# Holding TensorE's array mode longer, finishing a begun tile first, and one full-array product for the mask bias

## The chip, the cores and the metric

The kernel runs on one core of a Trainium2 chip. The metric is the device time of one execution in microseconds (us), taken as the median of the runs shown. A profiled execution stands beside them: it gives the instruction times from which everything below is read. The five engines are called PE (TensorE), DVE (VectorE), ACT (ScalarE), POOL (GpSimd) and SP (SyncE, which here only issues DMAs).

## The reference, cut to what matters

Four layers run one after the other on a sequence of 2048 rows of 512 numbers: A, B, A, B, each added to its own input. Layer A is attention over short segments with a memory that is handed from segment to segment; layer B is linear attention over the whole sequence.

```
def A(x, mem, ...):                       # layernorm before, residual after
    for s in range(64):                   # 64 segments of 32 rows
        h = concat(mem[8 rows], x[32 rows])
        q, k, v = h@Wq, h@Wk, h@Wv        # 32 heads of 128
        p = softmax(where(mask, q k^T * scale, -1e9))
        o = (p v) @ Wo
        mem = o[first 8 rows]             # goes into the next segment
        out = o[other 32 rows]
def B(x, ...):                            # linear attention, 32 heads of 16
    q, k, v = x@wqkv; phi(q), phi(k)
    out = (phi(q) (phi(k)^T v)) / (phi(q) sum phi(k)) @ wo
```

The mask lets the 8 memory rows see everything, and the others what is not later than they are. The chain that cannot be broken is the memory: segment s+1 cannot project its 8 memory rows before segment s has gone through projection, attention and output projection.

## The kernel before

**Work and staging.** All weights and x stay in SBUF. In layer A, "group" G is 128 rows (four segments, g = 0 to 3) and a segment s is one *turn* of the memory. Only 8+24 of a segment's 40 rows go through `project` in the turn; the last 8 rows of each of the four segments are collected into one "left-over" block of 32 rows, projected once per group by `left_block(G)`.

A projection (`project`, L630) uses the array as four independent 128x32 column strips: four products that run beside each other (here called a *pack*) and fill the 128 partitions of one PSUM bank with 8 heads by 4 strips. Four packs (one for each 128 input channels, c = 0 to 3) make a projection tile. `out_proj` (L808, eight packs) and the scores of the 32 segment rows (L759, L670) use the same strips. All this is called **column mode** below. Everything else on PE uses the array whole (**full mode**): transposes against the identity (L646), scores of the memory rows (L710), row sums by a product with ones (L722), probabilities times values (L735/L736 for the memory rows, L792/L793 for the others), the selection products L827 (picks the 8 memory rows out of the projected output and transposes them for the next turn) and L842/L847 (put segment rows back into place for the residual). The mask bias of the memory rows (`bias`, L701) is a third mode: two products with 16 of the 128 partitions contracted.

**A turn** is: project Q, K, V for two halves b = 0, 1; copy each tile out of PSUM into an image buffer `img` (`evac`, on ACT L498 or DVE L499); transpose it (L646) and copy it out again; bias, scores, exponential (L717, ACT), sums (L722), logarithm and exponential for the reciprocal (L725, L727, ACT), value products, multiply (L739, DVE); output projection (L808); copy; L827; copy into `hT`, from where the next turn's projections read. The 32 segment rows' attention (`x_attention`), the residual and the left-over block are filling work: nothing in the turn waits for them.

**What sets the order.** A list scheduler in the kernel (`_Prog.schedule`) writes each engine's order when the program is built. Each piece of work is a node with an assumed cost; `nd.tail` is the longest chain of assumed costs behind it. It steps through time, and on each engine takes the ready node with the largest tail. On PE it prefers a node of the mode that PE is in, as long as its tail is at most `MODE_SLACK` (0.3) below that of the best ready node; a switch is assumed to cost `PE_SWITCH` = 0.1. Nodes of a turn are `urgent`; a node that would open a new PSUM tile needs a free bank out of eight, and one that is not urgent needs three free. `after=early` on the bias ties it behind the copy of the K projection. On the chip the engines follow the written orders and wait for each other by semaphores; the assumed times are not used.

Image buffers: `img` has NI = 4 places, which `transposed` takes in turn for the memory turn and for the left-over block alike. The mask table `w16_sb` lies in a tensor of its own and is built once by POOL at the start (L542 to L547). Layer B lies in the same `arena` as layer A's buffers.

Of the kernel before, what the change touches and what calls it, by code (L numbers as in the profile page):

```python
# [18 lines left out]
MODE_SLACK = 0.3  # L19
# [35 lines left out]
class _Node:  # L55
    __slots__ = ("engs", "fn", "cost", "sync", "order", "tiles", "dsem", "dval", "eng", "start", "done",
                 "tail", "sig", "val", "waits", "know", "idx", "succ", "nleft", "urgent", "mode")


class _Prog:  # L60
# [17 lines left out]
    def add(self, engs, fn, cost, reads=(), writes=(), tiles=(), dsem=None, urgent=False, mode="full",  # L78
            after=()):
        nd = _Node()  # L80
        nd.mode = mode
        nd.engs = (engs,) if isinstance(engs, str) else tuple(engs)
# [12 lines left out]
        if dsem is not None:  # L95
            self.dma_tot[dsem] = self.dma_tot.get(dsem, 0) + 16
            nd.dval = self.dma_tot[dsem]
        for key in reads:
            st = self.res.setdefault(key, [None, []])
            if st[0] is not None:  # L100
                nd.sync.add(st[0])
            st[1].append(nd)
        for key in writes:
            st = self.res.setdefault(key, [None, []])
            if st[0] is not None and st[0] is not nd:
                nd.sync.add(st[0])
            for r in st[1]:
                if r is not nd:
                    nd.sync.add(r)
            st[0] = nd  # L110
            st[1] = []
        for tl in nd.tiles:
            if tl.ops:
                p = tl.ops[-1]
                if p.engs == ("pe",) and nd.engs == ("pe",):
                    nd.order.add(p)
                else:
                    nd.sync.add(p)
            tl.ops.append(nd)
        self.nodes.append(nd)  # L120
        return nd


    def schedule(self):
# [15 lines left out]
        for nd in reversed(nodes):  # L140
# [6 lines left out]
            nd.tail = best + min(nd.cost.values())  # L147
# [13 lines left out]
        n_left = len(nodes)  # L161
        pend = {e: [] for e in ENGINES}
# [34 lines left out]
        def pick_for(e):  # L197
            tn = self.now[e]
            while pend[e] and pend[e][0][0] <= tn + EPS:
                _, _, nd = heapq.heappop(pend[e])  # L200
                if nd.done is None:
                    heapq.heappush(ready[e], (-nd.tail, nd.idx, nd))
            pick = None
            kept = []
            while ready[e]:
# [4 lines left out]
                if first_of(nd):  # L210
                    bf = bank_for(tn)
                    if bf is None or bf[1] > tn + EPS or (not nd.urgent and n_free(tn) < 3):
                        kept.append(item)
                        continue
# [10 lines left out]
                elif nd.tail < pick.tail - MODE_SLACK:  # L225
# [12 lines left out]
        while n_left:  # L238
# [47 lines left out]
            nd.done = nd.start + nd.cost[e]  # L286
            self.now[e] = nd.done - (0.09 if e == "act" else 0.05 if e == "dve" else 0.0)
# [94 lines left out]
def _build_kernel(nc, A_x, A_mem0, A_Wq, A_Wk, A_Wv, A_Wo, A_seg_len, B_wqkv, B_wo, out):  # L382
# [35 lines left out]
    w16_sb = sb("w16_sb", [128, 4, 2, 32])  # L418
# [31 lines left out]
    img = av(NI * 512).rearrange("p (r x) -> p r x", r=NI)  # L450
# [14 lines left out]
    xlnA = av(D).rearrange("p (r x) -> p r x", r=1)  # L465

# [73 lines left out]

    BIG = -1.0e9
    pool(lambda g: g.memset(w16_sb[:, :, 0, :], 0.0), ["w16"])  # L542
    pool(lambda g: g.memset(w16_sb[:, :, 1, :], BIG), ["w16"])
    for gg in range(4):
        a = w16_sb[:, gg, 0, :]
        sel(a, GE, BIG, 0, [[-4, 4], [0, 8]], 1, "w16")
        sel(a, GE, BIG, 3, [[4, 4], [0, 8]], -1, "w16")  # L547
        sel(w16_sb[:, gg, 1, :], ALU.not_equal, 0.0, -gg, [[-4, 4], [0, 8]], 1, "w16")
# [71 lines left out]
    def a_layer(layer):  # L620
        img_no = [0]
# [68 lines left out]
        def mem_attention(s, b, early):  # L690
# [8 lines left out]
            def bias(pe):  # L699
                for a in range(2):  # L700
                    r = pe.matmul(tl.f32()[:, 128 * a:128 * a + 128], u16_sb[0:16, :],  # L701
                                  w16_sb[0:16, g, a, :].unsqueeze(1).to_broadcast([16, 4, 32]), start=(a == 0),
                                  stop=False, skip_group_check=True)
                return r
            add("pe", bias, c_pe(2, 128), reads=["u16", "w16"], tiles=[tl], urgent=True, after=early, mode="bias")
# [115 lines left out]
        def next_mem(s):  # L821
            G1, g1 = divmod(s + 1, 4)
            tl = P.tile()
            for h in range(2):
# [5 lines left out]
                add("pe", mm, c_pe(2, 128), reads=[(("outW", s % 3), h), "selm"], tiles=[tl], urgent=True)  # L830
# [5 lines left out]
        def residual(G, g):  # L836

            if g == 0:
# [5 lines left out]
                c_pe(1, 512), reads=[(("outW", w), 0), (("outW", w), 1), "selx"], tiles=[tl])  # L844
            if g == 3:
# [3 lines left out]
                    c_pe(1, 512), reads=[("outWl", 0), ("outWl", 1), "sell"], tiles=[tl])  # L849
# [195 lines left out]
```

## Time and profile before

| what | us |
|---|---|
| median of 3 runs | 2161.87 (2161.3 to 2163.71) |
| the profiled execution's own time | 2159.93 |
| its span, first to last instruction | 2158.2 |
| start until the first layernorm's transposes on PE | 48 |
| first layer A (48 to 1012) | 964 |
| first layer B (1012 to 1105) | 93 |
| second layer A (1105 to 2067) | 962 |
| second layer B (2067 to 2158) | 91 |

A view by stretches of time gives, for each, the busy time of every engine; a view of PE's instructions in order of time gives start and length of each row, with equal neighbours merged ("x8"). PE's matmuls overlap in the array, so the length of one is longer than the distance to the next: what a row costs is the distance from its start to the next row's start. In the four-group middle of a layer A the order repeats exactly every group.

### The profile page before, as it was taken

The numbers are of one execution on the slowest core, as the hardware profiler recorded it, in microseconds if no ns is written. First come the engines' busy times: TensorE is split into PE (matmuls) and PEld (weight loads), VectorE is DVE, ScalarE is ACT, GpSimd is POOL, SyncE is SP. The second block draws the span as 40 slices with busy tenths as digits, with TensorE's granted clock in tenths as the row PEclk, the third lists the DMA queues.
The fourth block names the chain that finished last, engine by engine and source line by source line (L and its number), as shares of the span: only waits on it lengthen the run. The fifth ranks groups of instructions, "written<-read, shape, count | busy, mean of one in ns | idle before, by whom it ended". The sixth has DMA issues, their size and how long they took to land.

```text
span 2158.2 us, 83024 instructions
## 1 busy us (share of the span) xinstructions
PE 2079.3 (96%) x37982; PEld 1163.5 (54%) x37982; DVE 1201.2 (56%) x3287; ACT 1159.7 (54%) x3112; POOL 14.8 (1%) x74
## 2 busy tenths in 40 slices
PE   1999999999999999998999999999999999999989
PEld 0555555555555555554655555555555555555545
DVE  0655555555554555556876555555555555554678
ACT  0555555555555555554645555555555555555554
POOL 2000000000000000000000000000000000000000
PEclk9999999999999999999999999999999999999999
DMA  9000000000000000001000000000000000000011
GB/s 350 3 3 2 3 3 3 3 3 3 3 3 3 3 3 3 3 3 41 1 2 3 3 3 3 3 2 3 3 3 3 3 3 3 3 3 3 3 41 40
DMA packets 12558, 30.48 MB, mean 14 GB/s; under 512 B 424, under 2 KB 9648, under 8 KB 10672
## 3 DMA queue, kind: packets, MB, share of 16 engines
q1 hardware_dynamic: 12208, 25.18, 3.2%
q8 instruction: 297, 4.87, 0.9%
q14 instruction: 53, 0.43, 0.1%
HBM read 23.08 MB, written 2.10 MB: 12 GB/s over the span
## 4 chain that ended last, share of the span: by engine, by line
PE 94%; DVE 2%; DMA 2%; ACT 1%; issue 0%; SPq 0%
PE pb L630 42%; PE pb L808 14%; PE pb L646 8%; PE pb L792 4%; PE pb L827 3%; PE pb L921 3%; PE pb L710 3%; PE pb L701 3%; PE pb L842 2%; PE pb L722 2%; DMA x_sb<-in_A_x_dram 2%; PE pb L735 2%; PE pb L759 2%; PE pb L914 1%; PE pb L736 1%; PE pb L771 1%
## 5 line engine op out<-in xcount | busy, mean ns | idle before, releaser
L498 ACT ACTIVATE arena_sb<-pb 128x512 bf16<-128x512 f32 (+6 forms) x1410 | 673.2, 492 | 458.7 <-PE pb L630 269.7
L630 PE MATMUL pb<-Wq_sb,arena_sb 128*32 128x512 bf16 x5120 | 478.2, 383 | 0.9 <-ACT arena_sb L498 0.4
L630 PE MATMUL pb<-Wk_sb,arena_sb 128*32 128x512 bf16 x5120 | 472.5, 382 | 0.0
L499 DVE CAST arena_sb<-pb 128x512 bf16<-128x512 f32 (+2 forms) x541 | 312.3, 578 | 237.6 <-PE pb L793 142.5
L630 PE MATMUL pb<-Wv_sb,arena_sb 128*32 128x512 bf16 x5120 | 374.4, 383 | 0.0
L808 PE MATMUL pb<-Wo_sb,arena_sb 128*32 128x512 bf16 x5184 | 350.1, 381 | 0.0
L780 DVE TENSOR_TENSOR arena_sb<-arena_sb 32x256 bf16<-32x256 bf16 x512 | 213.3, 417 | 133.6 <-ACT arena_sb L776 121.7
L499 DVE COPY arena_sb<-pb 128x512 bf16<-128x512 bf16 (+1 forms) x543 | 205.8, 399 | 137.8 <-PE pb L646 134.3
L646 PE MATMUL pb<-id_sb,arena_sb 128*128 128x128 bf16 x2560 | 216.7, 220 | 0.0
L630 PEld LDWEIGHTS pb<-Wq_sb,arena_sb 128*32 128x32 bf16 x5120 | 134.4, 96 | 133.2 <-ACT arena_sb L498 14.6
L646 PEld LDWEIGHTS pb<-id_sb,arena_sb 128*128 128x128 bf16 x2560 | 145.0, 97 | 103.2 <-issue 41.6
L630 PEld LDWEIGHTS pb<-Wk_sb,arena_sb 128*32 128x32 bf16 x5120 | 134.6, 97 | 108.5 <-issue 2.5
L717 ACT ACTIVATE arena_sb<-pb 128x256 bf16<-128x256 f32 x256 | 97.5, 381 | 158.9 <-PE pb L710 158.8
L498 ACT ACTIVATE outW_sb<-pb 128x256 fp32r<-128x256 f32 x198 | 75.8, 383 | 195.9 <-PE pb L808 194.5
L808 PEld LDWEIGHTS pb<-Wo_sb,arena_sb 128*32 128x32 bf16 x5184 | 119.7, 95 | 102.4 <-issue 20.7
L630 PEld LDWEIGHTS pb<-Wv_sb,arena_sb 128*32 128x32 bf16 x5120 | 109.6, 95 | 76.9
L782 DVE TENSOR_TENSOR arena_sb<-arena_sb 32x64 bf16<-32x64 bf16 x512 | 111.0, 217 | 15.8
L792 PE MATMUL pb<-arena_sb 128*128 128x128 bf16 x1024 | 115.2, 218 | 4.0 <-DVE arena_sb L782 4.0
L710 PE MATMUL pb<-arena_sb 128*128 128x32 bf16 x2048 | 118.6, 177 | 0.0
L499 DVE COPY arena_sb<-arena_sb 128x128 bf16<-128x128 bf16 x192 | 35.9, 194 | 128.8 <-PE pb L759 127.8
L793 PE MATMUL pb<-arena_sb 128*128 128x32 bf16 x1024 | 105.6, 178 | 0.0
L827 PEld LDWEIGHTS pb<-selm_sb,outW_sb 128*128 128x128 f32 x504 | 77.6, 188 | 51.8 <-ACT outW_sb L498 18.2
(108 smaller groups left out, 2330.6 us busy)
## 6 DMA issues: line engine op xcount, KB each, us to landing
Wq_sb<-in_A_Wq_dram SPq DMA_DIRECT2D x1, 4096.0 KB, 12.4
Wk_sb<-in_A_Wk_dram SPq DMA_DIRECT2D x1, 4096.0 KB, 22.2
Wv_sb<-in_A_Wv_dram SPq DMA_DIRECT2D x1, 4096.0 KB, 31.7
Wo_sb<-in_A_Wo_dram SPq DMA_DIRECT2D x1, 4096.0 KB, 43.2
arena_sb<-in_B_wqkv_dram SPq DMA_DIRECT2D x2, 1536.0 KB, 6.5
out_dram<-x_sb SPq DMA_DIRECT2D x16, 128.0 KB, 1.7
x_sb<-in_A_x_dram SPq DMA_DIRECT2D x1, 1920.0 KB, 11.5
arena_sb<-in_B_wo_dram SPq DMA_DIRECT2D x2, 512.0 KB, 7.5
```

Of the source, the lines that this page charges most:

```text
L498: return e.activation(o() if callable(o) else o, i() if callable(i) else i, ACTF.Copy)
L499: return e.tensor_copy(o() if callable(o) else o, i() if callable(i) else i)
L630: r = pe.matmul(tl.f32()[32 * j:32 * j + 32, 0:512], blk[:, c, :], W[:, c, o:o + 512], start=(c == 0), stop=(c == 3), tile_position=(0, 32 ...
L646: r = pe.transpose(tt.bf16()[:, 128 * i:128 * i + 128], img[:, k, 128 * i:128 * i + 128], id_sb[:, :])
L710: r = pe.matmul(tl.f32()[:, o:o + 32], kk[:, hh, :, :].rearrange("p j x -> p (j x)"), qT[:, r2, hh, :, 0:8], start=False, stop=True, skip_ ...
L717: add("act", lambda a: a.activation(Pm[:, k, :, :].rearrange("p a q -> p (a q)"), tl.f32()[:, 0:256], ACTF.Exp, scale=SCALE), c_act(256), ...
L780: add("dve", lambda v, q=q, j=j: v.tensor_tensor(Pbx[q, :, j, 0:32], Px[q, :, :], Rx[q, :, :], ALU.mult), c_dve(256), reads=["Px", "Rx"], ...
L782: add("dve", lambda v, q=q, j=j: v.tensor_tensor(Pbx[q, :, j, 32:40], PLL[q, g2, :, gl], Rx[q, :, 24:32], ALU.mult), c_dve(64), reads=[("P ...
L792: pe.matmul(o, vimg[:, r2, e], Pbx[:, hh, :, 0:32], start=True, stop=False)
L793: return pe.matmul(o[:, :, 24:32], vleft[:, g2, e], Pbx[:, hh, :, 32:40], start=False, stop=True)
L808: r = pe.matmul(tl.f32()[32 * j:32 * j + 32, :], oT[:, 4 * hh + j, :], Wo_sb[:, 8 * j + hh, :], start=(hh == 0), stop=(hh == 7), tile_posi ...
L827: r = pe.matmul(tl.f32()[:, 8 * c:8 * c + 8], outW[:, s % 3, 128 * c:128 * c + 128], selm_sb[:, :], start=True, stop=True)
```

## The change

1. `MODE_SLACK` goes from 0.3 to 2.0: PE may stay in its mode although a ready node of another mode has a chain that is up to 2.0 longer.
2. A node's rank is no longer its own tail alone (`prio`): a node gets at least the rank of the node before it on the same PSUM tile, so a projection, once begun, keeps the rank of its first pack.
3. The rule for opening a PSUM tile is rewritten: the oldest unopened tile needs one free bank, an urgent one two, any other three; a bank counts as free only when its last reader's signal has arrived.
4. The mask bias is one product over all 128 partitions and 256 columns instead of two with 16 partitions and 128 columns each; it counts as full mode. Its table `w16_sb` is now 128 by 4 by 2 by 128 numbers, lies in the arena and is built by POOL in each layer A.
5. The left-over block has two image buffers of its own; the memory turn keeps its four.
6. The assumed costs of L827 and of L842/L847 are raised (0.11 to 0.24 and 0.22 to 0.33). A field `lat` is added that nothing sets.

What is computed does not change.

```
-MODE_SLACK = 0.3
+MODE_SLACK = 2.0
...
+        for nd in nodes:
+            nd.prio = nd.tail
+            for tl in nd.tiles:
+                k = tl.ops.index(nd)
+                if k and tl.ops[k - 1] in nd.order and tl.ops[k - 1].done is None:
+                    nd.prio = max(nd.prio, tl.ops[k - 1].prio)
...
-                if own is None or (own.ops[-1].done is not None and own.ops[-1].done <= t_now):
+                lo = own.ops[-1] if own is not None else None
+                if lo is None or (lo.done is not None and lo.done + (PE_LAG if lo.eng == "pe" else HOP) <= t_now):
                     k += 1
...
-                    heapq.heappush(ready[e], (-nd.tail, nd.idx, nd))
+                    heapq.heappush(ready[e], (-nd.prio, nd.idx, nd))
...
-                    if bf is None or bf[1] > tn + EPS or (not nd.urgent and n_free(tn) < 3):
+                    while tiles[oldest[0]].bank is not None:
+                        oldest[0] += 1
+                    spare = 0 if tiles[oldest[0]] in nd.tiles else 1 if nd.urgent else 2
+                    if bf is None or bf[1] > tn + EPS or n_free(tn + EPS) <= spare:
...
-                elif nd.tail < pick.tail - MODE_SLACK:
+                elif nd.prio < pick.prio - MODE_SLACK:
                     kept.append(item)
                     break
...
-    img = av(NI * 512).rearrange("p (r x) -> p r x", r=NI)
+    img = av((NI + 2) * 512).rearrange("p (r x) -> p r x", r=NI + 2)
...
+    w16_sb = av(4 * 2 * 128).rearrange("p (g a h x) -> p g a h x", g=4, a=2, h=4)
...
-            k = img_no[0] % NI
-            img_no[0] += 1
+            k = img_no[0] % NI if urgent else NI + img_no[1] % 2
+            img_no[0 if urgent else 1] += 1
...
-            def bias(pe):
-                for a in range(2):
-                    r = pe.matmul(tl.f32()[:, 128 * a:128 * a + 128], u16_sb[0:16, :],
-                                  w16_sb[0:16, g, a, :].unsqueeze(1).to_broadcast([16, 4, 32]), start=(a == 0),
-                                  stop=False, skip_group_check=True)
-                return r
-            add("pe", bias, c_pe(2, 128), reads=["u16", "w16"], tiles=[tl], urgent=True, after=early, mode="bias")
+            add("pe", lambda pe: pe.matmul(tl.f32()[:, 0:256], u16_sb[:, :],
+                                           w16_sb[:, g, :, :, :].rearrange("p a h x -> p (a h x)"), start=True,
+                                           stop=False, skip_group_check=True),
+                c_pe(1, 256), reads=["u16", "w16"], tiles=[tl], urgent=True, after=early)
...
-                add("pe", mm, c_pe(2, 128), reads=[(("outW", s % 3), h), "selm"], tiles=[tl], urgent=True)
+                add("pe", mm, 0.24, reads=[(("outW", s % 3), h), "selm"], tiles=[tl], urgent=True)
...
+        BIG = -1.0e9
+        pool(lambda p: p.memset(w16_sb[:, :, 0, :, :], 0.0), ["w16"])
+        pool(lambda p: p.memset(w16_sb[:, :, 1, :, :], BIG), ["w16"])
+        for g in range(4):
+            sel(w16_sb[:, g, 0, :, :], GE, BIG, 0, [[0, 4], [-4, 4], [0, 8]], 1, "w16")
+            sel(w16_sb[:, g, 0, :, :], GE, BIG, 3, [[0, 4], [4, 4], [0, 8]], -1, "w16")
+            sel(w16_sb[:, g, 1, :, :], ALU.not_equal, 0.0, -g, [[0, 4], [-4, 4], [0, 8]], 1, "w16")
```

**How PE's order moves, place 1: the start of the attention in a turn of the steady part.** Rows are line, operation, output<-inputs, shape and count; "32x512" is column mode, everything else here full mode. `id_sb` marks a transpose, `w_sb,u_sb` the mask bias, "128x32" the memory rows' scores, `one_sb` their sums. Before:

```order
L646 MATMUL pb<-id_sb,arena_sb 128x128 x8
L630 MATMUL pb<-Wq_sb,arena_sb 32x512 x4
L630 MATMUL pb<-Wv_sb,arena_sb 32x512 x12
L701 MATMUL pb<-w_sb,u_sb 128x128 x2
L646 MATMUL pb<-id_sb,arena_sb 128x128 x4
L710 MATMUL pb<-arena_sb 128x32 x8
L630 MATMUL pb<-Wv_sb,arena_sb 32x512 x4
L630 MATMUL pb<-Wk_sb,arena_sb 32x512 x4
L646 MATMUL pb<-id_sb,arena_sb 128x128 x4
L722 MATMUL pb<-arena_sb,one_sb 128x128 x2
L630 MATMUL pb<-Wq_sb,arena_sb 32x512 x4
L630 MATMUL pb<-Wv_sb,arena_sb 32x512 x12
```

Now, at the same point of a turn (L639 is the old L630, L655 the old L646, L708 the bias, L716 the scores):

```order
L639 MATMUL pb<-Wk_sb,arena_sb 32x512 x16
L639 MATMUL pb<-Wv_sb,arena_sb 32x512 x32
L655 MATMUL pb<-id_sb,arena_sb 128x128 x8
L708 MATMUL pb<-arena_sb,u_sb 128x256
L655 MATMUL pb<-id_sb,arena_sb 128x128 x8
L716 MATMUL pb<-arena_sb 128x32 x4
L708 MATMUL pb<-arena_sb,u_sb 128x256
L639 MATMUL pb<-Wk_sb,arena_sb 32x512 x4
L716 MATMUL pb<-arena_sb 128x32 x12
```

Before, PE leaves the column mode three times in these rows besides the departure into the first one, and a fourth time into the second bias, which is the row behind them. Now it leaves it twice in a stretch that holds both biases: the value projections stand in one run of 32, and the transposes, the biases and the scores stand together.

**Place 2: the hand-over of the memory from one turn to the next.** `selm_sb,outW_sb` is the selection product L827 (now L833), after whose second pair and one copy the next turn's Q projection can start. Before:

```order
L808 MATMUL pb<-Wo_sb,arena_sb 32x512 x32
L759 MATMUL pb<-arena_sb 32x32 x32
L808 MATMUL pb<-Wo_sb,arena_sb 32x512 x12
L827 MATMUL pb<-selm_sb,outW_sb 128x8 x2
L808 MATMUL pb<-Wo_sb,arena_sb 32x512 x4
L827 MATMUL pb<-selm_sb,outW_sb 128x8 x2
L771 MATMUL pb<-arena_sb,bo_sb 128x256
L772 MATMUL pb<-arena_sb,bo_sb 128x8x8
L630 MATMUL pb<-Wq_sb,arena_sb 32x512 x4
L630 MATMUL pb<-Wk_sb,arena_sb 32x512 x4
L630 MATMUL pb<-Wq_sb,arena_sb 32x512 x4
```

Now (L814 is the old L808, L848 the old L842, L777/L778 the old L771/L772):

```order
L814 MATMUL pb<-Wo_sb,arena_sb 32x512 x32
L777 MATMUL pb<-arena_sb,bo_sb 128x256
L778 MATMUL pb<-arena_sb,bo_sb 128x8x8
L639 MATMUL pb<-Wk_sb,arena_sb 32x512 x8
L833 MATMUL pb<-selm_sb,outW_sb 128x8 x2
L639 MATMUL pb<-Wk_sb,arena_sb 32x512 x4
L848 MATMUL pb<-outW_sb,selx_sb 128x512
L833 MATMUL pb<-selm_sb,outW_sb 128x8 x2
L639 MATMUL pb<-Wk_sb,arena_sb 32x512 x8
L639 MATMUL pb<-Wq_sb,arena_sb 32x512 x16
```

The sums of the segment rows (L771/L772, now L777/L778) move ahead of the selection products, two packs of a left-over K projection stand between the last selection product and the next turn's Q projection, and the Q and K projections, which took turns pack by pack, now run one tile after the other.

Counted over the whole program, PE's order leaves the column mode 1,010 times before and 660 times now, and 256 pairs of bias products in the third mode become 256 single products in full mode.

More of the change, by code (lines that the diff above doesn't have):

```diff
@@ L56 @@
     __slots__ = ("engs", "fn", "cost", "sync", "order", "tiles", "dsem", "dval", "eng", "start", "done",
-                 "tail", "sig", "val", "waits", "know", "idx", "succ", "nleft", "urgent", "mode")
+                 "tail", "sig", "val", "waits", "know", "idx", "succ", "nleft", "urgent", "mode", "prio", "lat")
 class _Prog:
@@ L78, in add @@
     def add(self, engs, fn, cost, reads=(), writes=(), tiles=(), dsem=None, urgent=False, mode="full",
-            after=()):
+            after=(), lat=0.0):
         nd = _Node()
         nd.mode = mode
+        nd.lat = lat
         nd.engs = (engs,) if isinstance(engs, str) else tuple(engs)
@@ L146, in schedule @@
                     best = v
-            nd.tail = best + min(nd.cost.values())
+            nd.tail = best + min(nd.cost.values()) + nd.lat
+        for nd in nodes:
[4 more added lines that the diff above has]
+                    nd.prio = max(nd.prio, tl.ops[k - 1].prio)
         fenced = set()
@@ L161, in schedule @@
         n_left = len(nodes)
+        tiles = []
+        for nd in nodes:
+            for tl in nd.tiles:
+                if tl.ops[0] is nd:
+                    tiles.append(tl)
+        oldest = [0]
         pend = {e: [] for e in ENGINES}
@@ L285, in schedule @@
                 self.pe_mode = nd.mode
-            nd.done = nd.start + nd.cost[e]
-            self.now[e] = nd.done - (0.09 if e == "act" else 0.05 if e == "dve" else 0.0)
+            nd.done = nd.start + nd.cost[e] + nd.lat
+            self.now[e] = nd.start + nd.cost[e] - (0.09 if e == "act" else 0.05 if e == "dve" else 0.0)
             self.last[e] = nd
@@ L539, in _build_kernel @@
     sel(u16_sb[:, :], GE, 0.0, 7, [[-1, 128]], 8, "u16")
[L541 to L548, printed above, removed]
     pool(lambda g: g.memset(mx_sb[:, :], 1.0), ["mx"])
@@ L620, in a_layer @@
     def a_layer(layer):
-        img_no = [0]
+        img_no = [0, 0]
         cnt = {"m": 0}
@@ L843, in residual @@
                                            start=(g == 0), stop=False, skip_group_check=True),
-                c_pe(1, 512), reads=[(("outW", w), 0), (("outW", w), 1), "selx"], tiles=[tl])
+                0.33, reads=[(("outW", w), 0), (("outW", w), 1), "selx"], tiles=[tl])
             if g == 3:
```

3 lines of the change are left out of this document (1 added, 2 removed).

## The prediction

> **What bounds the kernel now.** First the page: its busy times, its slices and its chain.
>
> ```profile
> span 2158.2 us, 83024 instructions
> PE 2079.3 (96%) x37982; PEld 1163.5 (54%) x37982; DVE 1201.2 (56%) x3287; ACT 1159.7 (54%) x3112; POOL 14.8 (1%) x74
> ...
> PE 94%; DVE 2%; DMA 2%; ACT 1%; issue 0%; SPq 0%
> ```
>
> PE holds 94% of the chain that ended last; ACT and DVE are half empty. Since a busy PE need not be a PE at its peak, the stretches come next (columns: length, then busy time and count of PE, PEld, DVE, ACT, POOL, then clock).
>
> ```profile
> 48.00:1012.00 964.00, 961.01 (x18224) 531.99 (x18224) 521.34 (x1444) 532.00 (x1449) 0.00 (x0) 1.00 0.01 4
> 1012.00:1105.00 93.00, 79.69 (x774) 50.84 (x772) 79.52 (x201) 47.47 (x108) 0.21 (x2) 0.93 0.07 24
> 1105.00:2067.00 962.00, 959.18 (x18215) 530.38 (x18215) 520.88 (x1441) 531.59 (x1448) 0.00 (x0) 1.00 0.01 3
> ```
>
> The two layers A are 1926 of 2158 us, and PE lacks 3 us of busy time in each. The next row is one group, four turns, in the steady middle of the first layer.
>
> ```profile
> 183.20:243.10 59.90, 59.90 (x1142) 33.09 (x1138) 32.27 (x90) 33.55 (x91) 0.00 (x0) 1.00 0.01 3
> ```
>
> No gap at all, at full granted clock: 14.97 us a turn. The list of what PE waited for (total, times, longest) confirms it: its large rows are the start and layer B, and the largest one of a layer A is 4.0 us for two waits, at the layers' ends.
>
> ```profile
> PE pb L614 <- DVE arena_sb L607: 36.7, 4, 24.9
> PE pb L577 <- POOL arena_sb L524: 22.8, 1, 22.8
> ...
> PE pb L792 <- DVE arena_sb L782: 4.0, 2, 2.0
> ```
>
> So in a layer A time is what PE's rows cost one after the other, and a shorter row of rows is a shorter layer, until a wait appears.
>
> **What a change of mode costs.** These rows, in order of time, are from a turn of the first layer; a row's cost is the distance to the next start.
>
> ```profile
> 310.18 0.39 PE L630 MATMUL pb<-Wq_sb,arena_sb 128*32 128x512 bf16 x4
> 310.40 0.39 PE L630 MATMUL pb<-Wk_sb,arena_sb 128*32 128x512 bf16 x4
> 310.72 0.62 PE L646 MATMUL pb<-id_sb,arena_sb 128*128 128x128 bf16 x8
> 311.27 0.83 PE L630 MATMUL pb<-Wv_sb,arena_sb 128*32 128x512 bf16 x12
> 312.04 0.28 PE L701 MATMUL pb<-w_sb,u_sb 16*128 16x128 bf16 x2
> 312.25 0.40 PE L646 MATMUL pb<-id_sb,arena_sb 128*128 128x128 bf16 x4
> 312.48 0.25 PE L710 MATMUL pb<-arena_sb 128*128 128x32 bf16 x4
> 312.59 0.38 PE L646 MATMUL pb<-id_sb,arena_sb 128*128 128x128 bf16 x4
> 312.81 0.25 PE L710 MATMUL pb<-arena_sb 128*128 128x32 bf16 x4
> 312.99 1.05 PE L630 MATMUL pb<-Wv_sb,arena_sb 128*32 128x512 bf16 x16
> ...
> 314.30 0.27 PE L722 MATMUL pb<-arena_sb,one_sb 128*128 128x128 bf16 x2
> 314.41 0.25 PE L710 MATMUL pb<-arena_sb 128*128 128x32 bf16 x4
> ```
>
> A pack followed by a pack costs 0.22 (310.18 to 310.40); followed by a transpose it costs 0.32. Leaving the column mode is 0.10. Four transposes followed by full-mode work cost 0.22 (312.59 to 312.81), so eight 0.44; the eight before the V projection cost 0.55: the return is 0.11. Four score products cost 0.11 (312.48 to 312.59), but 0.18 before a projection: that return is 0.07. A round trip is thus 0.17 to 0.21, and I take 0.19. The bias pair costs 0.21 (312.04 to 312.25), the pair of sums, which has the same columns but stands in full mode, 0.11 (314.30 to 314.41): going from the bias mode to the full mode costs another 0.10. The way into the bias mode costs the same 0.10 or so as any departure (three packs, 311.27 to 312.04, are 0.77 where 3 x 0.22 are 0.66).
>
> The Trainium skill, TensorEngine Tiling (Array Packing), section Tiling Modes, says that changing the tiling mode drains the engine; TensorE: Matmul & The Clock Gate, section Step-by-step, puts that drain at about 128 cycles, an estimated 0.053 us at its 2.4 GHz. By that price the mode term below would be 350 x 0.106 + 254 x 0.053 = 51 us instead of 91. The rows show about twice the price at each of three kinds of change, so I go by the rows.
>
> **The change, part by part.** *Fewer changes of mode.* The order leaves the column mode 1,010 times now and 660 times after: 350 x 0.19 = 66 us, between 60 (at 0.17) and 74 (at 0.21). *The bias in full mode.* 254 of its 256 pairs stand between column and full mode: 254 x 0.10 = 25 us, between 23 and 28. The way in was counted above. Together 91, between 83 and 102.
>
> *The product itself.* One of 256 columns with 128 partitions contracted: the nearest row is L771, also 256 columns.
>
> ```profile
> 306.91 0.28 PE L771 MATMUL pb<-arena_sb,bo_sb 128*128 128x256 bf16 x1
> 307.03 0.19 PE L772 MATMUL pb<-arena_sb,bo_sb 128*128 128x64 bf16 x1
> ```
>
> It costs 0.12 against 0.11 for the pair in full mode: 256 x 0.01 = 3 us lost at most. Nor does each removed change give its mean: a selection product with four-byte operands hides part of one behind its long weight load. Going along the new order row by row, with each pair of neighbours at the distance that the same pair has in the trace (pairs that do not occur by the nearest kind), eight turns come to 114.7 us where two groups of before are 119.8: 5.1 us, and over 16 such stretches 82. I take 84, nearer to this than to 91, since it holds all pairs.
>
> *The order of finishing tiles, the bank rule, more mode slack.* They cost no rows; they shift when ACT and DVE get their work, and so can open waits. The hops that matter are at the end of a turn, where the tail of the layer shows one with nothing in between:
>
> ```profile
> 991.58 0.55 PE L827 MATMUL pb<-selm_sb,outW_sb 128*128 128x8 f32 x4
> ...
> 992.38 0.18 DVE L499 CAST arena_sb<-pb 128x32 bf16<-128x32 f32 x1
> ...
> 992.62 0.40 PE L630 MATMUL pb<-Wq_sb,arena_sb 128*32 128x512 bf16 x4 [0.15 <-DVE arena_sb L499]
> ```
>
> 0.25 from the product's end (992.13) to the copy, 0.18 copy, 0.06 to PE. The last selection product starts about 0.25 before its end, so its start and the next projection must be at least 0.74 apart, or some 0.6 where the quicker hop of the middle applies. In the new order the hand-over has two packs behind the last selection product: 0.18 + 0.43 = 0.61. That is at the edge; it costs 0 to 0.13 a turn. Going through the other waits of the steady part in the same way (producer's row, hop, time of the rows between), I find one in eight turns short by 0.23 and three by 0.03; near the layers' ends some of 0.2 to 0.7, as long as those there before. 16 x 0.3 = 5 us, and 3 for layer B, whose order also changes at places where DVE and ACT are behind: 8 us. The low end is 0; the high end, 0.3 a turn for queues on ACT and DVE that such a count does not see, is 128 x 0.3 = 38 us.
>
> *Left-over image buffers.* PE's list of waits has no row in layer A for an image buffer that was still in use: 0. Without the two places the left-over copies would share the four of the turn; what that would cost the trace does not show.
>
> *The mask table.* POOL builds it anew behind each layer B: two fills and 12 selections of 128x128.
>
> ```profile
> L524 POOL TENSOR_SCALAR_AFFINE_SELECT u_sb<-u_sb 128x128 bf16<-128x128 bf16 x2 | 0.6, 292 | 0.1
> L559 POOL MEMSET arena_sb<- 128x480 bf16 x1 | 0.5, 498 | 0.1
> ...
> 1117.23 0.28 PE L701 MATMUL pb<-w_sb,u_sb 16*128 16x128 bf16 x2
> ```
>
> 12 x 0.29 + 2 x 0.5 = 4.5 us, from 1105 on, while the projections of the first left-over block and turn run until the first bias at 1117.2: hidden with 7 us to spare, and POOL has nothing else queued there. Without this cover it would be 4.5 us, once. At the start POOL's list is ahead of x by far (the first layernorm product waits until 48 us for x).
>
> *The sum.* 2158.2 - 84 + 8 = 2082.2 us of span; the profiled execution's own time was 1.7 above its span: 2083.9. The runs' median is 1.9 above the profiled execution: **2086 us**. Own range: 2158.2 - 102 + 3.6 = 2060 if everything goes to the good end, 2158.2 - 80 + 38 + 3.6 = 2120 at the other; 2066 to 2112 is what I hold for this case.
>
> **Rivals.** *Half the gain goes into short waits* (chance 0.13, 2112 to 2140). Runs of 32 or 48 products of one mode leave copies in bunches: six projection tiles end within 5.2 us, and a copy takes 0.69 on DVE and 0.60 on ACT. For it: in the new order more waits have little room than before, and PE's order is fixed, so that it cannot do something else meanwhile. Against it: tiles that finish one after the other, each 0.87 us (four packs), give two copiers an even supply, where Q and K used to end 0.22 apart; ACT and DVE are 55% busy. At 0.33 us a turn it takes 42 us: 2086 + 34 = 2120.
>
> *The mode switch is cheaper when left out than it looks* (0.05): pairs overlap, only about half the price is saved, 2158.2 - 46 + 8 + 3.6 = 2124. Against it: the distances above are between starts on a PE without gaps. The price that the skill's drain gives, 51 us, ends near the same place, 2119.
>
> *PE is not the bound* (0.03, no change). Overlapping matmuls could look busy while something else sets their pace; PE would then only show gaps where the changes of mode were, and the time would stay at 2162. For it: weight loads keep PE's array for only 33.09 of a group's 59.90 us. Against it: the starts of the rows above follow from the rows themselves (0.22 a pack, 0.055 a transpose), and no wait ends in between. The Trainium skill, Perfetto Trace Analysis, section Identifying the Most-Contended Engine, has the rule that speaks for this rival: matmul busy time misjudges PE, and LDWEIGHTS busy, here 54%, shows its headroom.
>
> *The memory chain becomes the bound and the kernel gets slower* (0.05). Its rows (mean ns is the second number after the bar):
>
> ```profile
> L499 DVE COPY arena_sb<-pb 128x512 bf16<-128x512 bf16 x491 | 195.4, 420 | 136.0 <-PE pb L646 134.3
> L499 DVE CAST arena_sb<-pb 128x512 bf16<-128x512 f32 x283 | 194.9, 689 | 88.4 <-PE pb L630 83.7
> L717 ACT ACTIVATE arena_sb<-pb 128x256 bf16<-128x256 f32 x256 | 97.5, 381 | 158.9 <-PE pb L710 158.8
> L725 ACT ACTIVATE arena_sb<-pb 128x128 f32<-128x128 f32 x256 | 70.3, 275 | 56.1 <-PE pb L722 52.9
> L727 ACT ACTIVATE arena_sb<-arena_sb 128x128 f32<-128x128 f32 x256 | 80.1, 313 | 2.1
> L739 DVE TENSOR_TENSOR arena_sb<-pb,arena_sb 128x128 bf16<-128x128 f32 x256 | 74.1, 290 | 54.9 <-PE pb L736 51.0 <-PE pb L793 0.3 <-PE pb L722 0.2
> ```
>
> Copies and attention 2.4, the copies of the output (an estimate of 0.4 for 256 columns, from 0.69 for 512) and of the memory (0.18, above); on PE 16 packs of Q and K (3.5), the last four of the output projection (0.9), products between (0.6); some ten hops of 0.06 to 0.4, together 2: about 10 us of the 14.97. Holding a mode lets a ready link wait while up to 2.0 of rank difference is served. The chain crosses the mode border at four places a turn (projection to transposes, values to output projection, that to selection, selection to projection). From a mean hold of 1.2 us at each of them (10 + 4.8 = 14.8) it would end every turn later than PE's rows do; at 1.5 us it is 16.0 a turn, 128 x 1.0 above before: 2290. For it: a run of 32 V products (1.7 us) now stands ahead of the first transposes of a turn. Against it: the holds at the other borders are one or two packs, 0.2 to 0.4.
>
> **Chances and range.** Forecast 0.74, short waits 0.13, half price 0.05, no change 0.03, slower 0.05. The range 2064 to 2122 holds the forecast's case nearly whole and about half of the next two. A measurement of this kernel tells 0.2% (4 us) from no change. Faster: 0.74 + 0.13 + 0.05 = 0.92; same 0.03; slower 0.05.
>
> **What would show it.** The group of four turns at 57 to 58 us (two successive ones need not be alike) with PE still without gaps; eight transposes behind a projection still at 0.32 and 0.55 of distance; the new bias product at 0.12 among transposes; PE's waits in a layer A below 10 us in all; layer B at 91 to 95 us; POOL's second table done before the first bias of the second layer A. Wrong, if PE's waits within the layers A sum to over 40 us, if a change of mode costs something else where runs are long, or if a turn shows PE waiting for the copy behind the selection product each time.

## The result and the profile after

The changed kernel takes **2074.18 us** (median of 4 runs, 2072.74 to 2077.47), the kernel before 2161.59 (2160.55 to 2163.71): ratio 0.9597, 95% interval 0.958 to 0.9613, so 4.0% faster. The forecast was 2086 with a range of 2064 to 2122. One execution of another kernel below (the ring of six image buffers) took 4735 us with PE's rows over twice as long; it was the one with the profile, so that kernel is told by its other runs' times alone.

The page of the changed kernel: busy times and the chain that ended last, as shown of before.

```profile
span 2073.7 us, 82319 instructions
PE 1979.0 (95%) x37726; PEld 1188.5 (57%) x37726; DVE 1049.7 (51%) x3117; ACT 1305.0 (63%) x3282; POOL 23.6 (1%) x88
...
PE 89%; DVE 5%; DMA 2%; ACT 2%; issue 1%; SPq 0%; DVEq 0%
```

PE is still the engine that ends last, but its share of the chain fell from 94% to 89%, and DVE and ACT now hold 7%: turns have begun to wait for copies. Work also moved between the two copying engines, which no edit asks for: ACT from 1160 to 1305 us, DVE from 1201 to 1050. The stretches (length, busy time and count of PE, PEld, DVE, ACT, POOL, then clock):

```profile
48.00:967.60 919.60, 909.86 (x18096) 543.28 (x18096) 445.60 (x1359) 604.89 (x1534) 0.00 (x0) 1.00 0.01 4
967.60:1062.30 94.70, 79.53 (x777) 51.12 (x781) 79.71 (x201) 47.40 (x109) 3.69 (x10) 0.95 0.07 23
1062.30:1981.50 919.20, 909.91 (x18087) 542.77 (x18087) 444.61 (x1356) 604.30 (x1532) 2.50 (x7) 0.99 0.01 3
1981.50:2073.70 92.20, 79.38 (x769) 51.13 (x769) 75.87 (x193) 46.35 (x104) 0.21 (x2) 0.94 0.14 47
260.56:374.10 113.54, 112.89 (x2259) 67.50 (x2259) 56.24 (x172) 74.91 (x191) 0.00 (x0) 1.00 0.01 3
```

The layers A went from 964.0 to 919.6 and from 962.0 to 919.2, together 87 us; the layers B are 1.7 and 1.0 longer. The last row is eight turns of the steady part: 113.54 us, where before has 119.8. The order repeats every eight turns now, no longer every four.

What a change of mode costs has not changed. PE's rows in order of time (start, length, row), at the start of a turn's attention:

```profile
254.34 1.04 PE L639 MATMUL pb<-Wk_sb,arena_sb 128*32 128x512 bf16 x16
255.21 1.90 PE L639 MATMUL pb<-Wv_sb,arena_sb 128*32 128x512 bf16 x32
257.04 0.62 PE L655 MATMUL pb<-id_sb,arena_sb 128*128 128x128 bf16 x8
257.50 0.27 PE L708 MATMUL pb<-arena_sb,u_sb 128*128 128x256 bf16 x1
257.53 0.48 PE L848 MATMUL pb<-outW_sb,selx_sb 128*128 128x512 f32 x1
257.85 0.23 PE L798 MATMUL pb<-arena_sb 128*128 128x128 bf16 x1
```

Eight packs of V cost 1.83 from their start to the next row's (8 x 0.216 = 1.73 and one departure, 0.10). Eight transposes cost 0.46, without a return to the column mode behind them, and the bias starts without a change of mode ahead of it.

PE's waits, the largest ones (total, times, longest):

```profile
PE pb L798 <- DVE arena_sb L788: 4.4, 4, 2.0
PE pb L639 <- DVE arena_sb L517: 3.6, 12, 0.3
PE pb L853 <- DVE outWl_sb L517: 3.6, 12, 0.5
...
PE pb L728 <- ACT arena_sb L723: 1.7, 2, 0.9
PE pb L814 <- DVE arena_sb L745: 1.6, 6, 0.4
```

Two waits are new in the steady part, each once in eight turns: those of L639 and of L853 for a copy by L517. The first is at the hand-over of the memory:

```profile
265.78 0.59 PE L833 MATMUL pb<-selm_sb,outW_sb 128*128 128x8 f32 x4
266.23 0.48 PE L848 MATMUL pb<-outW_sb,selx_sb 128*128 128x512 f32 x1
266.35 0.71 DVE L788 TENSOR_TENSOR arena_sb<-arena_sb 32x64 bf16<-32x64 bf16 x3
266.63 0.40 PE L639 MATMUL pb<-Wq_sb,arena_sb 128*32 128x512 bf16 x4
267.09 0.19 DVE L517 CAST arena_sb<-pb 128x32 bf16<-128x32 f32 x1
267.32 0.22 DVE L788 TENSOR_TENSOR arena_sb<-arena_sb 32x64 bf16<-32x64 bf16 x1
267.34 0.83 PE L639 MATMUL pb<-Wq_sb,arena_sb 128*32 128x512 bf16 x12 [0.31 <-DVE arena_sb L517]
```

The selection product ends at 266.37, but the copy of the memory (L517, 128x32) stands behind three multiplies on DVE and starts at 267.09. PE issues one pack of a left-over projection and then nothing until 267.34. The bracket says 0.31 idle; the distance of the starts is 0.71 where a pack takes 0.22, so PE lost 0.49. The pack's row is 0.40 long, so the first 0.18 behind those 0.22 lie under it and do not show as idle time. The second is in front of the left-over output's selection product:

```profile
373.56 0.25 PE L716 MATMUL pb<-arena_sb 128*128 128x32 bf16 x4
373.63 0.41 DVE L517 CAST outWl_sb<-pb 128x256 fp32r<-128x256 f32 x1
374.10 0.50 PE L853 MATMUL pb<-outWl_sb,sell_sb 128*128 128x512 f32 x1 [0.28 <-DVE outWl_sb L517]
```

By idle time PE lacks 9.7 us in each layer A now (919.6 less 909.86), where before it lacked 3. Since short waits hide, I count waiting by distances too: for each row and its next, what exceeds the usual distance of that row before that mode (the 30th percentile over all kernels here) by more than 0.015 us. This gives 10 us in each layer A before and 19 after; in eight steady turns 0.7 and 1.3. How rows are merged and where the usual distance is set shifts all these levels together by some 4 us a layer; the differences between kernels are what is used below.

### The profile page after: what moved, and what is told of

It reads as the page before. It is cut to its first block, busy times and chain, and to the rows that moved or that the text cites. A ratio compares the mean times of both kernels' runs of the same rounds, so it can differ in the third digit from the quotient of the medians.

```text
span 2073.7 us, 82319 instructions
## 1 busy us (share of the span) xinstructions
PE 1979.0 (95%) x37726; PEld 1188.5 (57%) x37726; DVE 1049.7 (51%) x3117; ACT 1305.0 (63%) x3282; POOL 23.6 (1%) x88
## 4 chain that ended last, share of the span: by engine, by line
PE 89%; DVE 5%; DMA 2%; ACT 2%; issue 1%; SPq 0%; DVEq 0%
PE pb L639 42%; PE pb L814 13%; PE pb L655 7%; PE pb L798 3%; PE pb L935 3%; PE pb L833 3%; PE pb L716 2%; DVE arena_sb L786 2%; PE pb L848 2%; DMA x_sb<-in_A_x_dram 2%; PE pb L728 2%; PE pb L765 2%; PE pb L1002 1%; PE pb L928 1%; ACT arena_sb L516 1%; DVE arena_sb L788 1%
## 5 line engine op out<-in xcount | busy, mean ns | idle before, releaser
L516 ACT ACTIVATE arena_sb<-pb 128x512 bf16<-128x512 f32 (+6 forms) x1604 | 825.4, 519 | 451.9 <-PE pb L639 284.6
L517 DVE COPY arena_sb<-pb 128x512 bf16<-128x512 bf16 (+1 forms) x520 | 201.3, 407 | 529.5 <-PE pb L655 525.5
L639 PE MATMUL pb<-Wq_sb,arena_sb 128*32 128x512 bf16 x5120 | 351.4, 382 | 3.6 <-DVE arena_sb L517 3.6
L639 PE MATMUL pb<-Wk_sb,arena_sb 128*32 128x512 bf16 x5120 | 353.9, 382 | 0.6 <-ACT arena_sb L516 0.4
L814 PE MATMUL pb<-Wo_sb,arena_sb 128*32 128x512 bf16 x5184 | 337.1, 384 | 1.6 <-DVE arena_sb L745 1.6
L639 PE MATMUL pb<-Wv_sb,arena_sb 128*32 128x512 bf16 x5120 | 319.6, 380 | 0.0
L517 DVE CAST arena_sb<-pb 128x128 bf16<-128x128 f32 (+3 forms) x370 | 157.9, 429 | 137.4 <-PE pb L799 50.6
L639 PEld LDWEIGHTS pb<-Wv_sb,arena_sb 128*32 128x32 bf16 x5120 | 139.3, 97 | 129.4
L639 PEld LDWEIGHTS pb<-Wk_sb,arena_sb 128*32 128x32 bf16 x5120 | 138.6, 97 | 125.9 <-issue 2.4
L655 PE MATMUL pb<-id_sb,arena_sb 128*128 128x128 bf16 x2560 | 210.0, 220 | 0.0
L639 PEld LDWEIGHTS pb<-Wq_sb,arena_sb 128*32 128x32 bf16 x5120 | 129.0, 96 | 125.4 <-issue 12.7
L814 PEld LDWEIGHTS pb<-Wo_sb,arena_sb 128*32 128x32 bf16 x5184 | 126.8, 96 | 115.0 <-issue 10.9
L655 PEld LDWEIGHTS pb<-id_sb,arena_sb 128*128 128x128 bf16 x2560 | 151.4, 97 | 69.6 <-ACT arena_sb L516 48.8
L798 PE MATMUL pb<-arena_sb 128*128 128x128 bf16 x1024 | 124.5, 217 | 5.9 <-DVE arena_sb L788 4.4
L716 PE MATMUL pb<-arena_sb 128*128 128x32 bf16 x2048 | 110.0, 177 | 0.1
L716 PEld LDWEIGHTS pb<-arena_sb 128*128 128x128 bf16 x2048 | 81.8, 96 | 34.7 <-DVE arena_sb L517 14.9
L833 PEld LDWEIGHTS pb<-selm_sb,outW_sb 128*128 128x128 f32 x504 | 75.0, 189 | 46.0 <-ACT outW_sb L516 27.1
```

What stands on the lines that cost most here:

```text
L516: return e.activation(o() if callable(o) else o, i() if callable(i) else i, ACTF.Copy)
L517: return e.tensor_copy(o() if callable(o) else o, i() if callable(i) else i)
L639: r = pe.matmul(tl.f32()[32 * j:32 * j + 32, 0:512], blk[:, c, :], W[:, c, o:o + 512], start=(c == 0), stop=(c == 3), tile_position=(0, 32 ...
L655: r = pe.transpose(tt.bf16()[:, 128 * i:128 * i + 128], img[:, k, 128 * i:128 * i + 128], id_sb[:, :])
L716: r = pe.matmul(tl.f32()[:, o:o + 32], kk[:, hh, :, :].rearrange("p j x -> p (j x)"), qT[:, r2, hh, :, 0:8], start=False, stop=True, skip_ ...
L798: pe.matmul(o, vimg[:, r2, e], Pbx[:, hh, :, 0:32], start=True, stop=False)
```

## The experiments

Theory: time goes by the number of changes of the array's shape, 0.19 us for each departure from the column mode with its return and 0.08 to 0.10 for each change between bias and full mode; what PE waits comes on top. The rivals are told with each run. Departures are counted in the written order; "bias changes" are those between bias and full mode. Twelve kernels ran, four at a time on one chip beside the kernel before, which took 2161.8 each time.

| kernel | departures | bias changes | median us | ratio to before, 95% |
|---|---|---|---|---|
| before | 1,010 | 256 | 2161.6 | |
| before, bias in full mode | 1,006 | 0 | 2137.85 | 0.9888 (0.9871 to 0.9904) |
| before, slack 2.0 | 860 | 256 | 2131.56 | 0.986 (0.9843 to 0.9876) |
| changed | 660 | 0 | 2074.18 | 0.9597 (0.958 to 0.9613) |
| changed, bias of 16 partitions | 660 | 418 | 2110.27 | 0.9762 (0.9747 to 0.9776) |
| changed, slack 0.3 | 770 | 0 | 2105.07 | 0.9735 (0.972 to 0.9749) |
| changed, no finishing of tiles | 806 | 0 | 2102.44 | 0.9727 (0.9713 to 0.9742) |
| changed, old assumed costs | 678 | 0 | 2076.89 | 0.9609 (0.9595 to 0.9624) |
| changed, ring of four images | 626 | 0 | 2082.45 | 0.963 (0.9616 to 0.9645) |
| changed, ring of six images | 600 | 0 | 2080.21 | 0.9618 (0.9602 to 0.9634) |
| changed, DVE costs | 666 | 0 | 2079.71 | 0.9618 (0.9604 to 0.9633) |
| changed, slack 6.0 | 620 | 0 | **2062.76** | 0.9538 (0.9523 to 0.9554) |
| changed, DVE costs, slack 6.0 | 620 | 0 | 2062.15 | 0.9538 (0.9523 to 0.9552) |
| changed, DVE costs, ring of six, slack 4.0 | 572 | 0 | 2069.32 | 0.9566 (0.9552 to 0.958) |

**The third mode put back into the changed order.** All rows stand where they stood; only the number of partitions that the bias contracts differs.

```
-            ... u16_sb[:, :], w16_sb[:, g, :, :, :] ...
+            ... u16_sb[0:16, :], w16_sb[0:16, g, :, :, :] ...
```

> The changed kernel with its order untouched, but the one bias product of 256 columns contracts only the first 16 partitions (the others are zero, so the sum is the same). Theory (a change of the array's shape costs time, whatever the product's size): all 256 biases come from full-mode work in this order and 162 of them go back to it; entering costs 256 x 0.09 to 0.10, leaving to full mode 162 x 0.09 to 0.10, leaving to a projection was paid already: +38 to +42 us, about 2114 us. Rival (what was saved was the second product and the order around it, not the shape): 2074, within 4 us of the changed kernel.

Measured 2110.27, 36 us more. The same place of a turn in this kernel, PE's rows in order of time:

```profile
260.78 0.62 PE L655 MATMUL pb<-id_sb,arena_sb 128*128 128x128 bf16 x8
261.33 0.28 PE L708 MATMUL pb<-arena_sb,u_sb 16*128 16x256 bf16 x1
261.54 0.49 PE L848 MATMUL pb<-outW_sb,selx_sb 128*128 128x512 f32 x1
261.87 0.23 PE L798 MATMUL pb<-arena_sb 128*128 128x128 bf16 x1
```

From the transposes to the next value product are 1.09 us where the changed kernel has 0.81 (257.04 to 257.85), 0.28 for two changes at this place; on the mean over all 418 changes, 36 us are 0.09 each. A product that contracts 16 partitions among full ones is a mode of its own and is paid on the way in and out; the rival is out.

**The bias alone, in the order of before.** Two products as before, but all partitions and full mode.

```
-  ... u16_sb[0:16, :], w16_sb[0:16, g, a, :] ..., mode="bias")
+  ... u16_sb[:, :], w16_sb[:, g, a, :] ...)
```

> The kernel before with one edit: its two bias products contract all 128 partitions and count as full mode; 1,006 departures from the column mode instead of 1,010, and no third mode. Theory (shape): 254 changes from bias to full mode at 0.09 to 0.10 saved, 4 round trips at 0.19: 24 to 26 us less, 2136 us. Rival (shape is free, only the halved number of products matters): 2161, within 4 us of before.

Measured 2137.85, 24 us less, with as many products as before. So the gain of this edit is the shape; that one product took the place of two is not needed for it.

**Slack alone, in the kernel before.**

```
-MODE_SLACK = 0.3
+MODE_SLACK = 2.0
```

> The kernel before with the mode slack at 2.0 as its only edit. By its order 860 departures from the column mode instead of 1,010 (58 of them into the bias mode), 100 changes from full to bias mode instead of 2, 156 from bias to full instead of 254. Theory (changes): 150 x 0.19 = 28 us less, the bias changes even out: 2133. Rival (without finishing begun tiles a longer hold keeps tiles open and the chain late): 2150 or more, with PE's waits in the layers A above 15 us.

Measured 2131.56, 30 us less, near the count of 28, although waiting in a layer A is 16 us against 10.

**Slack undone in the changed kernel.** `MODE_SLACK` is 0.3 again, all other edits stay.

> The changed kernel with the mode slack back at 0.3. By the written order PE leaves the column mode 770 times instead of 660. Theory (number of changes): 110 x 0.19 = 21 us more, 2095 us. Rival (the slack costs as much in waits as it saves in changes): within 5 us of 2074, with fewer waits of PE in the layers A than the 11 or so of the changed kernel.

Measured 2105.07, 31 us more where the count says 21. The slack of 0.3 does not wait less: eight steady turns have 2.2 us of waiting (1.3 in the changed kernel), and PE's list has

```profile
PE pb L853 <- ACT outWl_sb L516: 8.4, 28, 0.3
PE pb L798 <- DVE arena_sb L788: 8.0, 34, 1.2
```

so these orders do not trade changes against waits; each order has its own waits. Over a whole layer A its waiting is only about 1 us above that of the changed kernel, so waits do not explain most of the 10 us above the count.

**No finishing of begun tiles.**

```
-                    nd.prio = max(nd.prio, tl.ops[k - 1].prio)
+                    pass
```

> The changed kernel with the rank of a node its own tail alone, as before: a begun tile is not finished first. By the written order 806 departures from the column mode instead of 660. Theory of changes alone: 146 x 0.19 = 28 us more, 2102. With waits at the rate of the run with slack 0.3 (31 us for 110 departures, 0.28 each): 2115. Rival (finishing tiles pays by earlier copies, not by changes): above 2120.

Measured 2102.44: the count to the microsecond. This edit works by the changes it avoids. That it is met so exactly is partly luck: this order waits some 4 us less in each layer A than the changed kernel, and its rows cost as much more than the count.

**Old assumed costs of the selection products.**

> The changed kernel with the old assumed costs of the selection products (0.11 and 0.22). By the written order 678 departures instead of 660: theory of changes alone 3 us more, 2077. Rival (the assumed costs matter by themselves: with too low ones the order asks for work before it is ready): over 2082, with PE's waits before the next turn's first projection (on the copies of ACT or DVE) above 10 us in all.

Measured 2076.89, as by the count. The difference to the changed kernel, 2.7 us, is within what these runs tell.

**Image buffers.** Shared by the turn and the left-over block: as before with four (`% NI`), and with all six (`% (NI + 2)`, shown here).

```
-            k = img_no[0] % NI if urgent else NI + img_no[1] % 2
-            img_no[0 if urgent else 1] += 1
+            k = img_no[0] % (NI + 2)
+            img_no[0] += 1
```

> The changed kernel, but the six image buffers are one ring that the turn's projections and the left-over block share. By the written order PE leaves the column mode 600 times instead of 660. Theory (time goes by the number of changes): 60 x 0.19 = 11 us less, 2063 us. Rival (buffers of their own keep the left-over block's copies out of the turn's way): PE's waits in the layers A grow by 10 us or more and the time is 2074 or above.

> The changed kernel with the four image buffers of before, shared by the turn and the left-over block. By the written order PE leaves the column mode 626 times instead of 660. Theory of changes alone: 34 x 0.19 = 6 us less, 2068. Theory with waits (after the ring of six, which took 2080 with 600 changes): sharing makes rows wait or moves work between ACT and DVE so that more is lost than saved, 2076 to 2090, and the difference to 2068 shows as waits of PE inside the layers A.

Both leave the column mode less often than the changed kernel and are slower, 2080.21 and 2082.45: 17 and 15 us above the count. In the ring of four the waiting in a layer A is 25 us (19), eight steady turns have 2.1 us, and most of what is added stands in front of the segment rows' value products:

```profile
PE pb L798 <- DVE arena_sb L788: 13.3, 30, 2.0
```

The value products wait for DVE's multiplies, 30 times instead of 4. Buffers of their own thus pay, though PE's list of before had no wait for them. This fits a scheduler that arranges the order around such a wait, so that the price appears elsewhere; no run shows that step by itself. The size is loose: the runs of the changed kernel reach from 2072.74 to 2077.47 and those of the ring of four from 2078.17 to 2083.82, and at the same granted clock of 0.991 the two are 4 us apart (2077.47 and 2081.31), not 8. The waits of the ring of six cannot be counted, so its 17 us are not assigned.

**Where the new waits come from.** The multiplies on DVE start 0.44 and 0.25 apart (four of them end after 1.75 and 0.96 us in the trace of before); the scheduler reckons 0.37 and 0.17.

```
-  c_dve(256), reads=["Px", "Rx"], ...      c_dve(64), reads=[("PLL", g2), "Rx"], ...
+  c_dve(256) + 0.065, ...                  c_dve(64) + 0.07, ...
```

> The changed kernel with two assumed costs raised to what the trace shows: the eight DVE multiplies of a turn start 0.44 and 0.24 apart there, where the scheduler reckons 0.37 and 0.17, so that DVE runs 0.5 us behind its plan in a turn and a copy behind the multiplies (the memory's, at 267.09 us) comes late. 666 departures from the column mode instead of 660: +1 us. Theory (waits of the changed kernel come from DVE's queue): PE's waiting in a layer A, measured as distances between starts above the usual one of the same pair, falls from 19 us to about 12 and the time to 2058 to 2064. Rival (waits only move to other rows): 2070 to 2078.

Measured 2079.71; waiting in a layer A 19 us, no less. The two new waits of the changed kernel, for L517 ahead of L639 and of L853, are gone from PE's list, and in their place stands

```profile
PE pb L728 <- ACT arena_sb L723: 5.3, 24, 0.8
```

The rival holds, with a time 2 us above its 2070 to 2078: DVE's lateness was real, but putting it right moved the waits to ACT's exponential.

**A longer hold.**

> The changed kernel with the mode slack at 6.0: 620 departures from the column mode instead of 660. Theory of changes alone: 40 x 0.19 = 8 us less, 2066. Rival (a hold of up to 6.0 makes the memory's chain late): more waiting of PE than 19 us in a layer A, 2074 or above.

> Both together: DVE costs as the trace shows them and mode slack 6.0, 620 departures. If the two theories add: 2074 - 8 - 12 = 2054. If a long hold needs waits: 2066 or above.

> DVE costs as the trace shows them, one ring of six image buffers, mode slack 4.0: 572 departures, the fewest found. Changes alone against the changed kernel: 88 x 0.19 = 17 us less, 2057; with waits reduced as in the theory of DVE's queue 2045. If a shared ring costs waits whatever the DVE costs (as the rings of four and six did, 8 to 17 us over the count): 2057 to 2070.

Slack 6.0 takes 2062.76, 11 us less than the changed kernel where the count gives 8; waiting in a layer A is 16 us against 19, so the rival of a late memory chain is out. **It beats both kernels.** With the DVE costs it is 2062.15, the same: the two theories do not add, since the first of them had fallen. The fewest changes, 572, give 2069.32: again a shared ring is above its count, with 22 us of waiting in a layer A.

**All together.** A least-squares line through the eleven kernels without a shared ring gives 0.190 us for a departure with its return and 0.082 for a bias change; ten of them lie within 5 us of it, slack 0.3 lies 10 above. The three with a shared ring lie 12 to 17 above.

This line mixes two things, since orders with fewer departures mostly wait longer. With the counted waiting of the layers A as a third term, a line through the thirteen kernels whose waits can be counted gives 0.21 us for a departure with its return, 0.094 for a bias change and about 1 us for each microsecond of waiting. No kernel lies more than 6 us off it; slack 0.3 is 3 above, the ring of four 0 and the ring of six with slack 4.0 4 above. The shared rings cost more than the count because they wait, and the price of a change is somewhat above 0.19.

The new rule for opening PSUM tiles was not undone by itself; what it contributes is not shown.

## Why the prediction was right, point by point

*What bounds the kernel.* Right. The time followed the rows that PE was spared, over a range of 100 us. That PE was no bound, the rival with the low share of weight loads, has fallen: PEld is busy 1188 us now, 57%, and the time fell with its share rising.

*Price of a change of mode.* Right in kind and near in size: 0.19 forecast, 0.190 by eleven kernels, 0.21 with the waiting taken out; 0.10 for bias to full forecast, 0.08 to 0.10 measured. The exact agreement at 0.190 is partly luck, since longer waits made up for a higher price. The case of half the price is out. The drain that the Trainium skill, TensorE: Matmul & The Clock Gate, section Step-by-step, puts at about 128 cycles comes to an estimated 0.053 us a change and 51 us for the two terms together. The runs do not agree with it as the price of a change: a departure measures 0.10 and a bias change 0.08 to 0.10.

*The sum over rows.* Too small, and this is the term that was mis-sized. I had 91 us by counting changes and 82 by going along the new order pair by pair, and took 84. The layers A are 87 us shorter although they wait 18 us longer, so distances without waiting fell by 105. The pairs' prices from before were at fault in part: some pairs occur there only at a layer's start, where they hold a wait. The only distance there of the layernorm's transposes to a column-mode row, 0.68 us, was used for rows that take 0.15; there are twelve of these, 6 us. At the price of 0.21 and 0.094 from all kernels the two terms come to 350 x 0.21 + 254 x 0.094 = 97, so most of the 14 us beyond the 91 are a price set too low. The rest I cannot assign; the selection products stand 0.128 apart on the mean before and 0.113 after, some 4 us, but part of that is counted as waiting above.

*New waits.* The mechanism was right, the size was not: 5 us forecast for the layers A (8 with layer B, within 0 to 38), 18 measured. Of the eight steady turns' waits I had found four by laying rows against hops, 0.3 us; the chip has 1.3, where before has 0.7 by the same counting. The hand-over's 0.49 is what such a laying-out misses: a copy that is short by itself behind a queue on DVE. The other place is L853, which waits 0.43 for the copy of the left-over output; I had 0.23 there. The hand-over with two packs behind the selection product, which I held to be at the edge, did not wait. The sign of waits below 10 us in a layer A was met by idle time alone (9.7), and not by distances (19).

*Image buffers.* Put at nothing, and wrong: undoing the edit costs 4 to 8 us, although it leaves the column mode 34 times less. PE's list of waits was silent on them, presumably because the order had been made with them.

*The mask table.* The cover held, the price did not:

```profile
1058.05 0.53 POOL L861 MEMSET arena_sb<- 128x512 bf16 x1 [88.97 <-DVE x_sb L1005]
...
1059.30 6.20 POOL L542 TENSOR_SCALAR_AFFINE_SELECT arena_sb<-arena_sb 128x128 bf16<-128x128 bf16 x12
...
1073.38 0.27 PE L708 MATMUL pb<-arena_sb,u_sb 128*128 128x256 bf16 x1
```

It took 7.5 us instead of 4.5, ending at 1065.5; the first bias of the second layer A is at 1073.38.

*Layer B.* 3 us forecast, 2.7 measured.

*The slower rival.* The memory's chain has not become the bound at a slack of 2.0, nor at 6.0, where the holds may be three times as long. The sums of the other rivals lay above 2110; none came.

Together: 105 saved, 18 lost in waits, 3 in layer B: 84 of span, where 76 were forecast. The two misses, 21 us of rows and 13 of waits, partly cancelled, and that is luck. The time came out 12 us from the forecast: 8.5 of span, and 3 because the median lay 1.3 below the profiled execution where the forecast put it 1.9 above.

## What to carry to other kernels

Where an engine has no gaps, read its price list from the distances between starts, and count changes of array shape like instructions: here one way cost as much as four small products of 0.025 us, and a product that contracts only 16 partitions was paid for on the way in and out. Prices of rare neighbours must be read where no wait hides in them. A price fitted to times alone holds whatever waiting came with it, here 0.19 instead of 0.21, so count the waits beside it. A resource that shows no wait in a scheduled kernel need not be free: the scheduler may have built the order around it, so undo it and let the order be made anew before calling it nothing.

## What the runs showed of the hardware that had not been expected

A selection (`affine_select`) of 128x128 with a pattern of three dimensions lasted 0.41 us on POOL, and 12 in a row took 6.20, 0.52 from start to start; the two 128x128 selections of `u_sb` before, with a pattern of one dimension, lasted 0.29 each, 0.36 from start to start. Part of a wait hides in the modelled length of a matmul: at the hand-over 0.31 of 0.49 us was shown as idle. And a bias product of 256 columns ahead of a four-byte product was followed after 0.03 us (257.50 to 257.53) instead of 0.11, with 0.32 behind that one: the distance to the next start is not always paid at the row that causes it.
